# Who requests the first loads, on which queue and in which type, in a one-core convolution and gated FFN kernel

## The chip, the cores and the metric

The kernel runs on one core of a Trainium2 chip. The metric is device time in microseconds (us), lower is better. A core has five engines with instruction streams of their own: TensorE (PE in the profile, its weight loads PEld), VectorE (DVE), ScalarE (ACT), GpSimd (POOL) and SyncE (SP). Transfers between memory and the core are requested by SP, ACT or POOL. Only POOL's requests convert fp32 to fp16 on the way in this kernel; what SP or ACT brings arrives as fp32.

## The reference

A softmax over 7 taps for each of 8 heads, a causal convolution over the sequence with these taps (24 channels a head), and a gated feed-forward layer:

```python
batch, seq, d_model = (8, 4096, 192); kernel_size = 7; n_heads = 8; d_ff = 1536
w = softmax(weight, axis=-1)                       # [8, 7]
x_pad = zeros of 6 rows ahead of x
out[b, s, h, g] = sum_k w[h, k] * x_pad[b, s + k, h, g]
x = out.reshape(32768, 192)
return (np.maximum(x @ w_gate, 0.0) * (x @ w_val)) @ w_out
```

## The kernel before

The batch is cut into two halves, the two *streams*, which are worked on side by side. The sequence is walked in 16 units of 1024 tokens a stream, each of two windows of 512. For each window `gate_val` loops over 12 chunks f of the hidden width: matmuls with the gate and value weights (line 562), relu on ACT (L573), the product on DVE (L574). Then `project` or `project_across` multiplies by `Wo` (L591, L675). PE is meant to run without a break.

The convolution of most units is made on DVE, ACT and POOL beside PE's work. That of the first unit's first window has nobody to hide behind and is made on PE: `conv_dense` (L382) multiplies rows of x with *bands*, matrices that hold the taps along a diagonal. This start is what the change is about. All of it is written out by hand; the program order of each engine is the order of the code.

The start, in the order of its parts:

- *Taps.* `wr` (8 x 7) is loaded. DVE takes the negated maximum (`mx`, L261), ACT the exponentials (`ex`, L264; a `spare` exponential at L144 loads the function table earlier), DVE the sum, its reciprocal and `soft` (L274 to L278). A matmul (L297) spreads `soft` over 112 rows, DVE multiplies it with a 0/1 mask `same` into `diag` (L307), and 14 matmuls with the 0/1 matrix `places` (L317) put the taps where the bands need them. DVE casts the bands from PSUM (`fill_band`, L347), in four pieces for heads 0 to 2, 3, 4 to 5 and 6 to 7. The masks come from `steps`, an iota of POOL, by shifts on DVE (`bits`, L250; `r_of`, L287).
- *x.* The first group has, for each stream, a block of first rows and a body of four pieces of 112 rows (`body`). The first stream's body (L131) and both streams' first rows (L132) come through SP as fp32 into a staging area (`stage`, in the buffer named `prods`) and are cast by ACT (L330, L148) and DVE (L148) into `x_h`. The second stream's body (L138) comes through POOL and is cast on the way.
- *Weights.* `load_w(s)` requests slice s of gate and value weights through POOL, as fp16, into the lower 64 partitions. The upper 64 get a copy (`both_halves`, L183): slices 0 and 1 by DVE, 2 to 5 by POOL (`pool_parts`, `pool_halves`). Slice 5 serves f = 9 to 11.
- *Warm-up.* `warm_up` issues matmuls of constants (L160) of the given widths, whose results nobody reads, to keep PE busy until x and the bands are there.

Of the kernel before, what the change touches and what calls it, by code (L numbers as in the profile page):

```python
# [8 lines left out]
FP = mybir.dt.float32  # L9
# [4 lines left out]
ALU = mybir.AluOpType  # L14
# [3 lines left out]
def kernel(  # L18
# [65 lines left out]
    def load_x(g):  # L84


        bp, toks = GROUPS[g]
        n, rows, step = len(toks), SUB if g < 2 else 128, toks[1] - toks[0]
        xt = xts[g] = x_room()
        for st in range(2):  # L90
            src = bass.AP(
                tensor=x.tensor,
                offset=x.offset + ((bp + NB * st) * S + toks[0] - PAD) * D,
                ap=[[D, rows], [step * D, n], [1, D]],
            )
# [11 lines left out]
    SEG = 16  # L107
    NSEG = SUB // SEG
    wr = const.tile([H, KW], FP)
    nc.sync.dma_start(out=wr[:], in_=weight)  # L110
# [13 lines left out]
    def body(st):  # L124
        return bass.AP(
            tensor=x.tensor,
            offset=x.offset + (NB * st * S + FIRST - PAD) * D,
            ap=[[D, SUB], [DSUB * D, GSUB - 1], [1, D]],
        )
# [5 lines left out]
            tensor=x.tensor, offset=x.offset, ap=[[D, FIRST], [NB * S * D, 2], [1, D]]  # L135
        ),
    )
    nc.gpsimd.dma_start(out=xts[0][0:SUB, 1:GSUB, 1, :], in_=body(1))  # L138
    steps = const.tile([SUB, 64], I32)
    nc.gpsimd.iota(steps[:], pattern=[[1, 64]], base=0, channel_multiplier=64)  # L140
    ones = const.tile([H, 1], FP)
# [1 line left out]
    spare = const.tile([H, 1], FP)  # L143
    nc.scalar.activation(spare[:], ones[:], ACTF.Exp)  # L144
    nc.vector.memset(stage(0, PAD, 0, 2, 0, 1), 0.0)

    def first_rows(copy, cols):
        copy(  # L148
# [9 lines left out]
    def warm_up(*widths):  # L158
        for n, w in enumerate(widths):
            nc.tensor.matmul(  # L160
                out=warm[:, n % 2, 0:w], lhsT=busy[:, 0:128], rhs=busy[:, 0:w], start=True, stop=True
            )

    warm_up(512, 512, 512, 512, 512, 512, 128)

# [4 lines left out]
    Wo = const.tile([128, NFF, D], F16)  # L170
    CUTS = [0, 128, 384, 640, 896, 1152, DFF]

    def load_w(s, which=3):
        cols = slice(CUTS[s], CUTS[s + 1])
        for src, dst in ((moe_w_gate, Wg), (moe_w_val, Wv))[which == 2 : 1 + (which > 1)]:
            nc.gpsimd.dma_start(
                out=dst[0:64, :, cols],
                in_=src.rearrange("(c p) f -> p c f", p=64)[:, :, cols],
            )

    def both_halves(copy, s, dst):
        cols = slice(CUTS[s], CUTS[s + 1])
# [19 lines left out]
    def lane_load(v, hold=None):  # L202


        xe = epool.tile([128, TILES, 2, NCH, 64], F16, name="x_e")
        xes[v] = xe
        for j0, n, t in pieces(v):
            bp, t0 = t // S, t % S
            start = int(t0 == 0)
            if start:  # L210
                nc.gpsimd.memset(xe[0:HALO, j0, :, :, :], 0.0)
            for st in range(2):
                b = bp + NB * st
                first = nc.gpsimd.dma_start(  # L214
                    out=xe[:, j0 + start : j0 + n, st, :, :].rearrange("p j c r -> p j (c r)"),
                    in_=bass.AP(
                        tensor=x.tensor,
                        offset=x.offset + (b * S + t0 - HALO + 128 * start) * D,
                        ap=[[D, 128], [128 * D, n - start], [1, D]],
                    ),  # L220
                )
                if hold is not None:
                    tc.add_manual_dep(first.ins, hold.ins.name, SYNC, reason="behind the turns of the lane before")
                    hold = None
                if start:
# [7 lines left out]
    load_w(1)  # L233
    load_w(2)
    load_rest(load_x(1))
    load_w(3)
    pool_parts(2)
    load_w(4)
    load_w(5)
    pool_halves(3)  # L240
    lane = lane_load(1)
    next(lane)

    ex = const.tile([H, KW + 1], FP)
    nc.vector.memset(ex[:, KW : KW + 1], 1e-9)

# [1 line left out]
    def bits(src, n, down, keep):  # L248
# [8 lines left out]
        )  # L257
        return out

    mx = const.tile([H, 1], FP)  # L260
    nc.vector.tensor_reduce(  # L261
        out=mx[:], in_=wr[:], axis=mybir.AxisListType.X, op=ALU.max, negate=True
    )
    nc.scalar.activation(ex[:, 0:KW], wr[:], ACTF.Exp, bias=mx[:])  # L264
    NROW = SEG + KW - 1
    s_of = bits(steps[:, 0:1], 1, 6, SEG - 1)
    col = bits(steps[:, 0:NROW], NROW, 0, 63)
# [1 line left out]
    with nc.allow_low_precision("zero and one"):  # L269
        nc.vector.tensor_tensor(  # L270
            out=same[:], in0=col[:, 0:SEG], in1=s_of[:].to_broadcast([SUB, SEG]), op=ALU.is_equal
        )
    sm = const.tile([H, 1], FP)
    nc.vector.tensor_reduce(out=sm[:], in_=ex[:], axis=mybir.AxisListType.X, op=ALU.add)  # L274
    nc.vector.reciprocal(sm[:], sm[:])
    soft = const.tile([H, KW, SEG], F16)
    with nc.allow_low_precision("rounded as the band is"):
# [4 lines left out]
            scalar2=None,  # L282
            op0=ALU.mult,
        )
    k_of = bits(steps[:, 0:1], 1, 10, 7)
    r_of = const.tile([SUB, 1], FP)
    nc.vector.tensor_tensor(out=r_of[:], in0=s_of[:], in1=k_of[:], op=ALU.add)  # L287
    with nc.allow_low_precision("zero and one"):
        nc.vector.tensor_scalar(
            out=places[:, SUB - SEG : SUB - SEG + NROW],  # L290
            in0=col[:],
            scalar1=r_of[:],
            scalar2=None,
            op0=ALU.is_equal,
        )
    spread = psum.tile([128, 2, 512], FP, name="ps")
    nc.tensor.matmul(  # L297
        out=spread[0:SUB, 0, 0:H],
# [2 lines left out]
        start=True,  # L301
        stop=True,
    )
    warm_up(512)
    diag = const.tile([SUB, H, SEG], F16)
    with nc.allow_low_precision("products with one and zero"):
        nc.vector.tensor_tensor(  # L307
# [15 lines left out]
                skip_group_check=True,  # L323
            )

    warm_up(512, 256)

    for c in range(NCH):
        cols = slice(64 * c, 64 * c + 64)
        nc.scalar.copy(  # L330
            out=xts[0][0:ROWS0, 1:GSUB, 0, cols],
            in_=stage(0, ROWS0, 0, 1, 1, GSUB - 1)[:, :, cols],
        )
# [586 lines left out]
```

## Time and profile before

| | |
|---|---|
| median of 3 runs | 761.83 us (761.78 to 762.53) |
| profiled execution, its own time | 761.75 us |
| its span, first to last instruction | 760.0 us |
| PE, DVE, ACT, POOL busy | 756.0, 707.8, 617.9, 404.2 us |
| granted TensorE clock, mean | 1.000 |
| first convolution matmul (L382) starts | 5.57 us |
| first gate matmul (L562) starts | 7.29 us |
| one f step of a later window (18.12 to 19.42) | 1.30 us |

A row of the timeline has the start in us, the duration in us, the engine, the line, the operation, what is written and read, the shapes and how often; in square brackets stands how long the engine was idle before and what ended that. SPq and ACTq are queues for transfers; a transfer's row there is only its issue. The list of DMA issues gives the size of a transfer and the us from its issue to its landing. "+1 forms" means that a group has rows of other shapes in it.

### The profile page before, as it was taken

What the parts mean: (1) busy time and instruction counts of PE and PEld (TensorE: products, weight loads), DVE (VectorE), ACT (ScalarE), POOL (GpSimd) and SP (SyncE); (2) the same over time, 40 slices, a digit from 0 to 9 for tenths busy, and PEclk for the clock granted to TensorE, in tenths of its full rate; (3) what the DMA queues carried; (4) which work ended last, traced back from release to release, by engine and by line L of the source; (5) the groups of instructions that cost most, each with busy time, mean ns of one, the idle gap of its engine ahead of it and who ended that gap; (6) DMA issues with size and microseconds to landing.
All of it is one profiled execution on the core that took longest, in us unless ns stands there. A gap on an engine that the chain in (4) does not pass through costs nothing.

```text
span 760.0 us, 30644 instructions
## 1 busy us (share of the span) xinstructions
PE 756.0 (99%) x13637; PEld 461.6 (61%) x13637; DVE 707.8 (93%) x769; ACT 617.9 (81%) x722; POOL 404.2 (53%) x262
## 2 busy tenths in 40 slices
PE   9999999999999999999999999999999999999998
PEld 5595555555555555556555565666666666666548
DVE  7998999999999999999999999999999999999891
ACT  6787887978879798897988879788798887976671
POOL 8519449094580936819276291863908548091000
PEclk9999999999999999999999999999999999999999
DMA  9969029588395894949659498593957939754832
GB/s 131 119 116 140 13 68 169 150 105 183 94 184 146 99 172 105 199 119 134 167 93 184 119 151 167 87 181 113 170 145 104 187 94 157 146 109 109 185 88 85
DMA packets 231452, 100.41 MB, mean 132 GB/s; under 512 B 185240, under 2 KB 220568, under 8 KB 231320
## 3 DMA queue, kind: packets, MB, share of 16 engines
q1 hardware_dynamic: 190280, 82.93, 53.5%
q0 software_dynamic: 40896, 15.50, 19.6%
q8 instruction: 106, 1.74, 1.0%
q14 instruction: 26, 0.21, 0.1%
q10 hardware_dynamic: 144, 0.03, 0.0%
HBM read 31.48 MB, written 47.19 MB: 104 GB/s over the span
## 4 chain that ended last, share of the span: by engine, by line
PE 99%; POOL 0%; DVE 0%; issue 0%; ACT 0%; POOLq 0%
PE ps L562 66%; PE ps L675 29%; PE ps L591 3%; PE ps L642 1%; PE ps L382 0%; PE ps L160 0%; POOL x_h L138 0%; PE ps L317 0%; PE ps L423 0%; DVE bits L250 0%; DVE soft L278 0%; PE ps L297 0%; POOL steps L140 0%; ACT acc L650 0%; DVE same L270 0%
## 5 line engine op out<-in xcount | busy, mean ns | idle before, releaser
L574 DVE TENSOR_TENSOR hT<-gr,ps 128x1024 f16<-128x1024 f16 (+1 forms) x386 | 469.0, 1216 | 29.7 <-ACT gr L573 3.1
L573 ACT ACTIVATE gr<-ps 128x1024 f16<-128x1024 f32 (+1 forms) x386 | 393.3, 1020 | 100.6 <-PE ps L562 100.4
L510 POOL TENSOR_TENSOR prods<-prods 128x1344 f32<-128x1344 f32 x70 | 213.0, 3043 | 268.8 <-DVE prods L506 265.4
L562 PE MATMUL ps<-xc,Wg 64*64 64x512 f16 (+1 forms) x4320 | 318.8, 376 | 0.0
L562 PE MATMUL ps<-xc,Wv 64*64 64x512 f16 (+1 forms) x4320 | 318.7, 376 | 0.0
L675 PE MATMUL ps<-hT,Wo 64*64 64x512 f16 x4032 | 220.1, 376 | 0.0
L562 PEld LDWEIGHTS <-Wv 64*64 64x64 f16 (+1 forms) x4320 | 149.0, 105 | 99.5 <-issue 0.2
L562 PEld LDWEIGHTS <-Wg 64*64 64x64 f16 (+1 forms) x4320 | 145.0, 106 | 103.8 <-issue 0.6
L675 PEld LDWEIGHTS <-Wo 64*64 64x64 f16 x4032 | 130.4, 107 | 87.2
L534 DVE SCALAR_TENSOR_TENSOR acc<-x_r,tap,acc 128x576 f32<-128x576 f16 x225 | 165.3, 812 | 0.0
L504 ACT ACTIVATE prods<-x_r,tap 128x448 f32<-128x448 f16 x222 | 127.2, 659 | 0.0
L697 ACT COPY x_h<-ps 128x2048 uint16<-128x2048 uint16 x28 | 51.8, 1848 | 8.8 <-PE ps L675 8.8
L214 POOL DMA_DIRECT2D x_e<-in_x_dram x58 | 47.0, 818 | 12.4 <-ACT acc L520 12.2
L484 POOL COPY x_p<-x_e 128x960 f16<-128x960 f16 (+1 forms) x58 | 50.4, 913 | 0.0
L510 POOL TENSOR_TENSOR xc<-prods 128x1344 f16<-128x1344 f32 x14 | 42.6, 3040 | 1.1
L697 POOL COPY y<-x_h 128x2048 uint16<-128x2048 uint16 x14 | 26.6, 1898 | 23.3 <-ACT x_h L753 23.3
L534 DVE SCALAR_TENSOR_TENSOR xc<-x_r,tap,acc 128x576 f16<-128x576 f16 x45 | 34.1, 812 | 0.0
L520 ACT ACTIVATE acc<-x_r,tap 128x576 f32<-128x576 f16 x45 | 31.4, 764 | 0.0
L506 DVE TENSOR_SCALAR prods<-x_r,tap 128x448 f32<-128x448 f16 x70 | 27.6, 447 | 0.0
L591 PE MATMUL ps<-Wo,hT 64*128 64x192 f16 x576 | 24.6, 243 | 0.0
L591 PEld LDWEIGHTS <-hT 64*128 64x128 f16 x576 | 24.0, 94 | 0.4
L753 ACT COPY x_h<-ps 128x512 f32<-128x512 f32 x14 | 8.2, 587 | 10.9 <-ACT x_h L697 5.5
(65 smaller groups left out, 92.5 us busy)
## 6 DMA issues: line engine op xcount, KB each, us to landing
out_dram<-out_s SPq DMA_DIRECT2D x62, 384.0 KB, 3.6
held<-x_h SPq DMA_DIRECT2D x14, 512.0 KB, 3.3
held<-x_h SPq DMA_DIRECT2D x28, 256.0 KB, 3.2
held<-y SPq DMA_DIRECT2D x14, 512.0 KB, 5.0
x_e<-in_x_dram POOLq DMA_DIRECT2D x34, 192.0 KB, 6.4
x_e<-in_x_dram POOLq DMA_DIRECT2D x24, 240.0 KB, 5.1
x_r<-x_p SPq DMA_TRANSPOSE x131, 5.2
out_s<-held SPq DMA_TRANSPOSE x56, 5.5
```

The source lines that it names most:

```text
L214: first = nc.gpsimd.dma_start(out=xe[:, j0 + start : j0 + n, st, :, :].rearrange("p j c r -> p j (c r)"), in_=bass.AP(tensor=x.tensor, off ...
L484: nc.gpsimd.tensor_copy(out=xp[:, j0 : j0 + n, :, st, :], in_=xe[:, j0 : j0 + n, st, :, :])
L504: engine.activation(out=out, in_=in_, func=ACTF.Copy, scale=scale)
L510: nc.gpsimd.tensor_tensor(out=pr[:, 0] if k < KW - 1 else xc[v + 1][:, :, LDVE:UNIT], in0=pr[:, 0], in1=pr[:, k], op=ALU.add,)
L520: nc.scalar.activation(out=accs[v][:, c, :], in_=shifted(v, c, 0, 0), func=ACTF.Copy, scale=tap[:, c, 0:1],)
L534: nc.vector.scalar_tensor_tensor(out=xc[v][:, c, 0:LDVE] if k == KW - 1 else acc[:, c, :], in0=shifted(v, c, k, 0), scalar=tap[:, c, k : k ...
L562: nc.tensor.matmul(out=pss[i][m : m + M, st, :], lhsT=W[64 * st : 64 * st + 64, c, 128 * f + m : 128 * f + m + M], rhs=xcb[64 * st : 64 * ...
L573: nc.scalar.activation(out=gr[:, sts], in_=pss[0][:, sts], func=ACTF.Relu)
L574: nc.vector.tensor_tensor(out=h[:, f, sts], in0=gr[:, sts], in1=pss[1][:, sts], op=ALU.mult)
L591: mm = nc.tensor.matmul(out=outs[q], lhsT=h[64 * r : 64 * r + 64, f, st, 128 * q : 128 * (q + 1)], rhs=Wo[64 * r : 64 * r + 64, f, :], sta ...
L675: mm = nc.tensor.matmul(out=ps[bank][64 * half : 64 * half + 64], lhsT=Wo[64 * r : 64 * r + 64, f, d : d + 64], rhs=hs[w][64 * r : 64 * r ...
L697: copy(out=pt[:], in_=src[:].bitcast(U16).rearrange("p b (t l) -> p b l t", l=2))
```

## The change

The taps' request moves from SP to ACT. The second stream's body moves from POOL, which cast it on the way, to SP, as fp32 into the staging area, and is cast there by ACT in three pieces; of the first stream's body, one piece of three moves from ACT to DVE, and the cast of the first rows on DVE now stands ahead of the bands. POOL's first weight request gets a wait for the taps' maximum. The masks and `places` stand ahead of that maximum on DVE. Three warm-ups change their widths.

```diff
-    nc.sync.dma_start(out=wr[:], in_=weight)
+    nc.scalar.dma_start(out=wr[:], in_=weight)
...
-    nc.gpsimd.dma_start(out=xts[0][0:SUB, 1:GSUB, 1, :], in_=body(1))
+    nc.sync.dma_start(out=stage(0, SUB, 1, 1, 1, GSUB - 1), in_=body(1))
...
+    def first_x(copy, st, c0, c1):
+        copy(
+            out=xts[0][0:ROWS0, 1:GSUB, st, 64 * c0 : 64 * c1],
+            in_=stage(0, ROWS0, st, 1, 1, GSUB - 1)[:, :, 64 * c0 : 64 * c1],
+        )
...
-    warm_up(512, 512, 512, 512, 512, 512, 128)
+    warm_up(512, 512, 512, 512, 512, 512, 384)
...
-    def load_w(s, which=3):
+    def load_w(s, which=3, hold=None):
...
-            nc.gpsimd.dma_start(
+            first = nc.gpsimd.dma_start(
...
+            if hold is not None:
+                tc.add_manual_dep(first.ins, hold.ins.name, SYNC, reason="behind the first x")
+                hold = None
...
-    load_w(0)
+    top = nc.vector.tensor_reduce(
+        out=mx[:], in_=wr[:], axis=mybir.AxisListType.X, op=ALU.max, negate=True
+    )
+    nc.scalar.activation(ex[:, 0:KW], wr[:], ACTF.Exp, bias=mx[:])
+    load_w(0, hold=top)
...
-    warm_up(512)
+    warm_up(512, 128)
...
-    warm_up(512, 256)
-
+    warm_up(512)
+
+    first_x(nc.scalar.copy, 0, 0, 1)
+    first_rows(nc.scalar.copy, slice(0, 64))
+    first_x(nc.scalar.copy, 0, 2, 3)
     for c in range(NCH):
-        cols = slice(64 * c, 64 * c + 64)
-        nc.scalar.copy(
-            out=xts[0][0:ROWS0, 1:GSUB, 0, cols],
-            in_=stage(0, ROWS0, 0, 1, 1, GSUB - 1)[:, :, cols],
-        )
-        if c == 0:
-            first_rows(nc.scalar.copy, cols)
+        first_x(nc.scalar.copy, 1, c, c + 1)
+    first_x(nc.vector.tensor_copy, 0, 1, 2)
+    first_rows(nc.vector.tensor_copy, slice(64, D))
...
     fill_band(1, [4, 5], nc.vector.tensor_copy)
-    first_rows(nc.vector.tensor_copy, slice(64, D))
     fill_band(1, [6, 7], nc.vector.tensor_copy)
```

How the instructions stand, at three places. First DVE, from the product `diag` to the first weight copy. Before (`band` is cast from the PSUM tile `ps`, `prods` is the staging area):

```order
L307 TENSOR_TENSOR diag<-ps,same 112x128 [waits PE_49]
L347 CAST band_188<-ps 128x336 [waits PE_49]
L347 CAST band_190<-ps 128x112
L347 CAST band_192<-ps 128x224 [waits PE_49]
L148 CAST x_h<-prods 102x2x128 [waits DMAHW2_49]
L347 CAST band_195<-ps 128x224
L183 COPY Wg<-Wg 64x3x128 [waits DMASW1_49]
```

DVE, the same place now:

```order
L316 TENSOR_TENSOR diag<-ps,same 112x128 [waits PE_49]
L148 CAST x_h<-prods 110x4x64 [waits DMAHW1_49]
L154 CAST x_h<-prods 102x2x128 [waits DMAHW2_49]
L355 CAST band_192<-ps 128x336 [waits PE_49]
L355 CAST band_194<-ps 128x112
L355 CAST band_196<-ps 128x224 [waits PE_49]
L355 CAST band_198<-ps 128x224
L192 COPY Wg<-Wg 64x3x128 [waits DMASW0_49]
```

A cast of the first body is new, and it and the first rows' cast, each behind a transfer of SP's, stand ahead of all four bands.

Second POOL, from the start of the program. Before:

```order
L138 DMA x_h<-in_x_dram 112x4x192
L140 ISA
L140 IOTA steps 112x64
L176 DMA Wg<-in_moe_w_gate_dram 64x3x128
L176 DMA Wv<-in_moe_w_val_dram 64x3x128
L176 DMA Wg<-in_moe_w_gate_dram 64x3x256
```

POOL, the same place now:

```order
L140 ISA
L140 IOTA steps 112x64
L182 DMA Wg<-in_moe_w_gate_dram 64x3x128 [waits DVE_49]
L182 DMA Wv<-in_moe_w_val_dram 64x3x128
L182 DMA Wg<-in_moe_w_gate_dram 64x3x256
```

The body's transfer is gone from the head of the queue, and the first weight request waits for DVE, with all that follows on POOL behind it.

Third ACT, from the start of the program to the first casts of PSUM. Before:

```order
L144 ACT_TABLE_LOAD
L144 ACTIVATE spare<-ones 8x1 [waits DVE_49]
L264 ACTIVATE ex<-wr,mx 8x7 [waits DMAHW0_49,DVE_49]
L330 CAST x_h<-prods 110x4x64 [waits DMAHW1_49]
L148 CAST x_h<-prods 102x2x64 [waits DMAHW2_49]
L330 CAST x_h<-prods 110x4x64 x2
L400 CAST xc<-ps 128x512 [waits PE_49] x2
```

ACT, the same place now:

```order
L110 DMA wr<-in_weight_dram 8x7
L144 ACT_TABLE_LOAD
L144 ACTIVATE spare<-ones 8x1 [waits DVE_49]
L280 ACTIVATE ex<-wr,mx 8x7 [waits DMAHW0_49,DVE_49]
L148 CAST x_h<-prods 110x4x64 [waits DMAHW1_49]
L154 CAST x_h<-prods 102x2x64 [waits DMAHW2_49]
L148 CAST x_h<-prods 110x4x64
L148 CAST x_h<-prods 110x4x64 [waits DMAHW3_49]
L148 CAST x_h<-prods 110x4x64 x2
L407 CAST xc<-ps 128x512 [waits PE_49] x2
```

The taps' request stands ahead of the table load, and three casts of the second stream's body, behind SP's third transfer, ahead of the first `xc`.

More of the change, by code (lines that the diff above doesn't have):

```diff
@@ L230, in lane_load @@
                 yield
-    load_w(0)
[L233 to L242, printed above, removed]
     ex = const.tile([H, KW + 1], FP)
@@ L258, in bits @@
         return out
-    mx = const.tile([H, 1], FP)
-    nc.vector.tensor_reduce(
-        out=mx[:], in_=wr[:], axis=mybir.AxisListType.X, op=ALU.max, negate=True
-    )
-    nc.scalar.activation(ex[:, 0:KW], wr[:], ACTF.Exp, bias=mx[:])
     NROW = SEG + KW - 1
@@ L272 @@
         )
+    k_of = bits(steps[:, 0:1], 1, 10, 7)
+    r_of = const.tile([SUB, 1], FP)
+    nc.vector.tensor_tensor(out=r_of[:], in0=s_of[:], in1=k_of[:], op=ALU.add)
+    with nc.allow_low_precision("zero and one"):
+        nc.vector.tensor_scalar(
+            out=places[:, SUB - SEG : SUB - SEG + NROW],
+            in0=col[:],
+            scalar1=r_of[:],
+            scalar2=None,
+            op0=ALU.is_equal,
+        )
+    mx = const.tile([H, 1], FP)
+    top = nc.vector.tensor_reduce(
+        out=mx[:], in_=wr[:], axis=mybir.AxisListType.X, op=ALU.max, negate=True
+    )
+    nc.scalar.activation(ex[:, 0:KW], wr[:], ACTF.Exp, bias=mx[:])
+    load_w(0, hold=top)
+    load_w(1)
+    load_w(2)
+    load_rest(load_x(1))
+    load_w(3)
+    pool_parts(2)
+    load_w(4)
+    load_w(5)
+    pool_halves(3)
+    lane = lane_load(1)
+    next(lane)
     sm = const.tile([H, 1], FP)
@@ L284 @@
         )
[L285 to L295, printed above, removed]
     spread = psum.tile([128, 2, 512], FP, name="ps")
@@ L324 @@
             )
-    warm_up(512, 256)
+    warm_up(512)
+    first_x(nc.scalar.copy, 0, 0, 1)
+    first_rows(nc.scalar.copy, slice(0, 64))
+    first_x(nc.scalar.copy, 0, 2, 3)
     for c in range(NCH):
-        cols = slice(64 * c, 64 * c + 64)
-        nc.scalar.copy(
-            out=xts[0][0:ROWS0, 1:GSUB, 0, cols],
-            in_=stage(0, ROWS0, 0, 1, 1, GSUB - 1)[:, :, cols],
-        )
-        if c == 0:
-            first_rows(nc.scalar.copy, cols)
+        first_x(nc.scalar.copy, 1, c, c + 1)
+    first_x(nc.vector.tensor_copy, 0, 1, 2)
+    first_rows(nc.vector.tensor_copy, slice(64, D))
     bands, wide_bands, ends = {}, {}, []
```

## The prediction

> **What bounds the kernel now.** I read the page first: the share of each engine and the chain that ended last.
>
> ```profile
> PE 756.0 (99%) x13637; PEld 461.6 (61%) x13637; DVE 707.8 (93%) x769; ACT 617.9 (81%) x722; POOL 404.2 (53%) x262
> PE 99%; POOL 0%; DVE 0%; issue 0%; ACT 0%; POOLq 0%
> ```
>
> TensorE (PE) carries 99% of the chain, so a change counts only if it moves PE's first useful matmul or opens a gap behind it. The timeline shows both ends of that question: the first convolution matmul (L382), and the pace of the gate and value matmuls (L562) afterwards.
>
> ```profile
> 5.57 1.78 PE L382 MATMUL ps<-band,x_h 110*32 110x104 f16 x120
> 18.12 0.81 PE L562 MATMUL ps<-xc,Wg 64*128 64x512 f16 x6
> 19.42 0.81 PE L562 MATMUL ps<-xc,Wg 64*128 64x512 f16 x6
> ```
>
> One step of the f loop takes 19.42 - 18.12 = 1.30 us for six pairs of 512 columns, 0.22 us a pair, and nothing else stands between. The edits lie wholly before about 21 us, so the time follows the start of L382 (5.57) and any new gap in the next 16 us. What could be won in all is little: no step shown below ends early enough to let L382 start before about 5.4.
>
> What feeds L382? The timeline of each engine, in order of time:
>
> ```profile
> 0.74 0.41 SPq L110 DMA_DIRECT2D wr<-in_weight_dram  x1
> 0.74 1.28 ACT L144 ACT_TABLE_LOAD   x1 [0.74 <-PEq L904]
> 1.21 0.34 SPq L131 DMA_DIRECT2D prods<-in_x_dram  x1
> 1.31 0.88 POOL L138 DMA_DIRECT2D x_h<-in_x_dram  x1 [0.87 <-POOLq L904]
> 1.36 0.06 DVE L245 MEMSET ex<- 8x1 f32 x1
> 1.59 0.48 SPq L132 DMA_DIRECT2D prods<-in_x_dram  x1
> 2.03 0.20 ACT L144 ACTIVATE spare<-ones 8x1 f32<-8x1 f32 x1
> 2.10 0.15 DVE L261 TENSOR_REDUCE mx<-wr 8x1 f32<-8x7 f32 x1 [0.67 <-DMA wr<-in_weight_dram]
> 2.28 0.30 ACT L264 ACTIVATE ex<-wr,mx 8x7 f32<-8x7 f32 x1
> 2.28 0.22 POOL L140 IOTA steps<- 112x64 int32 x1
> 2.41 0.68 POOL L176 DMA_DIRECT2D Wg<-in_moe_w_gate_dram  x1
> 2.53 0.24 DVE L250 TENSOR_SCALAR bits<-steps 112x1 int32<-112x1 int32 x2 [0.29 <-POOL steps L140]
> 2.81 0.17 DVE L270 TENSOR_TENSOR same<-bits,bits 112x16 f16<-112x16 int32 x1
> 2.90 0.14 DVE L274 TENSOR_REDUCE sm<-ex 8x1 f32<-8x8 f32 x1
> 3.26 0.32 DVE L278 TENSOR_SCALAR soft<-ex,sm 8x112 f16<-8x112 f32 x1
> 3.51 0.13 DVE L250 TENSOR_SCALAR bits<-steps 112x1 int32<-112x1 int32 x1
> 3.63 0.25 PE L297 MATMUL ps<-same,soft 8*112 8x8 f16 x1
> 3.82 0.61 PE L160 MATMUL ps<-const-bfloat16-1.0 128*128 128x512 bf16 x1
> 4.02 0.28 DVE L307 TENSOR_TENSOR diag<-ps,same 112x128 f16<-112x128 f32 x1
> 4.35 0.91 PE L317 MATMUL ps<-diag,places 112*128 112x64 f16 x14
> 4.59 0.41 ACT L330 CAST x_h<-prods 110x256 f16<-110x256 f32 x1 [2.01 <-DMA prods<-in_x_dram]
> 4.92 0.51 DVE L347 CAST band<-ps 128x336 f16<-128x336 f32 x1 [0.62 <-PE ps L317]
> 5.10 0.30 ACT L148 CAST x_h<-prods 102x128 f16<-102x128 f32 x1
> 5.83 0.45 DVE L148 CAST x_h<-prods 102x256 f16<-102x256 f32 x1
> ```
>
> Three things must be there. The first band is written by 4.92 + 0.51 = 5.43. The casts of the first stream's x on ScalarE (ACT) end at 5.10 + 0.30 = 5.40. The second stream's x comes through GpSimd's (POOL's) cast transfer, whose landing the list of DMA issues gives:
>
> ```profile
> x_h<-in_x_dram POOLq DMA_DIRECT2D x1, 168.0 KB, 4.3
> prods<-in_x_dram SPq DMA_DIRECT2D x1, 144.0 KB, 3.5
> ```
>
> Issued at 1.31 it lands at about 1.31 + 4.3 = 5.6, just where L382 starts. Softmax, staged x and second x thus end within 0.2 us of each other; taking one away uncovers the next.
>
> **The change part by part.** *Requests.* With the taps gone from SyncE's (SP's) queue, the first body goes out at 0.74 instead of 1.21. The first rows follow 0.38 us later (1.59 - 1.21), at 1.12, and the second body at about 1.12 + 0.48 + 0.04 = 1.65, behind both. The first body landed 4.59 - 1.21 = 3.4 us after its issue, so now at 4.1; the first rows at 1.12 + 3.5 = 4.6. For the second body the nearest rows give 1.65 + 3.4 = 5.05 at best and, at POOL's 4.3, 5.95 at worst. I take 5.15, nearer SP's rows, because it is now the same kind of transfer on the same queue, as a volume check bears out:
>
> ```profile
> 3.00:3.50 0.50, 0.50 (x3) 0.02 (x1) 0.43 (x3) 0.00 (x0) 0.50 (x2) 1.00 1.07 362
> 4.00:4.50 0.50, 0.50 (x5) 0.25 (x5) 0.30 (x2) 0.00 (x0) 0.50 (x2) 1.00 1.44 226
> 4.50:5.00 0.50, 0.50 (x13) 0.50 (x12) 0.08 (x1) 0.41 (x1) 0.50 (x2) 1.00 1.61 191
> ```
>
> The last column is GB/s. The x transfers run at 362 once they flow, near 3.0, or 2.5 with the requests 0.47 earlier. All three together are 336 + 144 + 336 = 816 KB, 0.84 MB, or 2.3 us at that rate: done at 4.8, plus some tenths to be reported.
>
> The Trainium skill (DMA: Bandwidth & Descriptors, "Issuing engines are not separate DMA queues") speaks against the move: transfers of all issuers run on the same 16 engines, and another issuer saves only issue time. By that, the fp32 second body, twice the bytes written, would gain nothing from its new queue, and the sum would come to case C below.
>
> *Taps' chain.* On ACT the request (0.41, the SP row's) stands ahead of the table load: 0.74 + 0.47 = 1.21, + 1.28 + 0.20 = 2.7 for the end of `spare`. On POOL the iota loses the 0.88 us transfer ahead of it and ends at about 1.5 if it starts where that transfer did. On VectorE (DVE) the bits, `same`, second bits, `r_of` and `places` come ahead of the maximum: 2.53 to 2.98, and 3.51 to 4.02, which is 0.45 + 0.5 = 0.95 us; started at 1.42 to 1.6, they end at 2.4 to 2.55. The maximum (0.15; the taps having landed at 2.10, if ACT's queue is as quick as SP's) ends at 2.55 to 2.7. So `ex` starts at 2.7, not 2.28. From `ex`'s end to `soft`'s end takes 3.58 - 2.58 = 1.0 in the trace, but 0.32 of it was DVE busy with `bits` and `same` (2.58 to 2.90), so now 0.68 + 0.02: `soft` ends at 2.7 + 0.3 + 0.7 = 3.7 instead of 3.58. Of the 0.42 us lost at `ex`, 0.3 is given back.
>
> *Bands.* L297's matmul moves to 3.74, and the 512-column warm-up 0.19 behind it. Those 512 columns take 0.43 us at the slow clock and the added 128 another 0.11, so L317's place matmuls start near 3.93 + 0.54 = 4.47, not 4.35: +0.12. `diag` stays hidden (about 4.05 to 4.33). DVE then has two casts in place of one before the first band: the x cast (256 elements, like the 0.45 us row at 5.83, which takes 0.37 of DVE before the next starts) from 4.36, the first rows from 4.73 (landed at 4.6), done at 5.1; PSUM is ready at 4.92 + 0.12 = 5.04. So the band is cast from 5.1 to 5.6. Both casts are hidden by 0.06 us short of all; if the first rows land late, every tenth counts in full.
>
> *ACT's casts.* First piece 4.12, rows 4.65, third piece 4.95, then the second stream's first piece from 5.25 to 5.65. L382 starts at about 5.65: **+0.08**. The rest of these casts and bands are due later, at 0.6 us for each third of L382.
>
> *Weights.* The first weight issue waits for the maximum: 2.6 to 2.75 instead of 2.41, **+0.2 to +0.35**, and everything queued behind it on POOL moves with it: six weight transfers, x of the next group, the half copies. Who waits for POOL last is seen here:
>
> ```profile
> 20.09 1.16 POOL L183 COPY Wv<-Wv 64x1152 f16<-64x1152 f16 x1
> 21.15 0.53 PEld L562 LDWEIGHTS <-Wv 64*128 64x128 f16 x6
> ```
>
> The copy ends at 21.25, in the middle of the weight loads that use it: no cover. POOL late by 0.2 to 0.35 against PE late by 0.08 leaves 0.1 to 0.27; against it stands the second body's cast, gone from POOL's stream. I take **+0.12**. Below nothing the weights bring no gain, as PE is then full.
>
> *Sum.* +0.08 + 0.12 = +0.2 us. The profiled execution took 761.75 (span 760.0 and 1.75 around it), 0.08 under the median of 761.83. So 761.95 by that execution, **762.0** as a median.
>
> **The rivals.** *A, forecast (0.55):* as summed, 762.0.
>
> *B, a small gain (0.20).* PE is let through as soon as `diag` is there, the casts hide, and the lighter POOL stream keeps the half copies on time: band at 4.92, L382 at 5.43 to 5.45. That is -0.12, up to -0.3 with less loss inside the block: 761.6.
>
> *C, x late (0.12).* One SP queue now holds all of it. At 226 GB/s, the rate of the rows in which weights run beside x, 0.84 MB takes 3.7 us from 2.5: 6.2, plus the 0.41 cast, L382 at 6.65: +1.1, 762.9. At the 191 of the next row it is 6.9 and +1.75. It decides once the second body lands after 5.25. Against it: the hold keeps the weights out until then. With the landing at 5.95, from POOL's row, L382 would start near 6.4, for 762.7. The section of the Trainium skill named above (DMA: Bandwidth & Descriptors) is the rule behind this case.
>
> *D, the clock comes late (0.10), slower.* The lines by form show when PE speeds up, though the granted clock column says 1.00 throughout:
>
> ```profile
> L160 PE MATMUL ps<-const-bfloat16-1.0 128*128 128x512 bf16 x1 | 0.6, 607 | 0.0
> L160 PE MATMUL ps<-const-bfloat16-1.0 128*128 128x512 bf16 x1 | 0.5, 461 | 0.0
> ```
>
> The 512-column matmul at 3.82 took 607 ns, the one at 5.07 461: the switch falls near 5.2, 4.4 us after the first warm-up (0.78). If the wait ahead of L297 starts this anew, 4.4 us from 3.9 is 8.3; work from 5.65 to 8.3 at half pace costs 1.3 us: 763.1 to 763.3. It is beyond 0.2% if full pace comes after 8.7, to which I give half of this chance. For it: the wait moves; against it: the warm-up grows from 128 to 384 columns just there (0.21 us at the slow pace), covering the 0.11 us move.
>
> The Trainium skill (TensorE: Matmul & The Clock Gate, "Part 1: The HAM clock gate") has the clock follow a free-running window of some 3.4 us of activity. By that, the switch could only slip by a whole window, 5.2 to 8.6, for an estimated 1.5 us and 763.4; no row here shows the window itself.
>
> *E, the edits do nothing (0.03).* If POOL's first instruction comes so late that the weights would go out at 2.6 anyway, the hold is empty and all covers hold: 761.8.
>
> **How the numbers follow.** The likeliest case gives 762.0. The range runs from B's far end (761.5), less 0.2 since each landing in it is known to a tenth or two, to D's first price: 761.3 to 763.1. Left out are C's worse end and half of D, about 0.1. For this kernel 0.2% is 1.5 us, about what a measurement can tell from no change: 760.3 to 763.35. Slower by more needs the late half of D (0.05), C at 191 GB/s (0.04), or something unpriced (0.04): 0.13. Faster by more would need L382 at 4.05, before the first body has landed: 0.02. The rest, 0.85, lies within.
>
> **What the profile after would show.** Right: L382 starts at 5.55 to 5.75, its release an ACT cast of the second stream or a band; the maximum at 2.4 to 2.55 and the first weights at 2.6 to 2.75; the last value weights' copy ending near 21.5 with a small gap on PE; one f step still 1.30. Wrong: the second body landing after 5.3 (C), the last warm-up ahead of L382 still at 607 ns for 512 columns (D), or PE gaps beyond 22 us, of which I foresee none.

## The result: slower by 0.22%

The changed kernel took 763.93 us (median of 13 runs, 762.94 to 766.0), the kernel before 762.33 beside it (13 runs, 761.78 to 763.23): ratio 1.0022, interval 1.0015 to 1.0029, or 1.1 to 2.2 us. Forecast were 762.0 and a range up to 763.1. The profiled execution took 763.40, with a span of 761.6.

The page of the changed kernel, its first line of busy time and the chain that ended last:

```profile
PE 756.7 (99%) x13637; PEld 492.0 (65%) x13637; DVE 708.5 (93%) x770; ACT 618.6 (81%) x724; POOL 403.0 (53%) x261
PE 99%; DMA 1%; SPq 0%; ACT 0%; issue 0%
```

TensorE still carries the chain, but ahead of it stands a transfer where before stood POOL's iota and DVE's masks. PE's waits over the first 25 us say where it stood still; the kernel before has only the first 0.8 of the program's start:

```profile
PE ps L389 <- ACT x_h L148: 0.8, 1, 0.8
PE ps L166 <- PEq L911: 0.8, 1, 0.8
PE ps L389 <- DVE band L355: 0.2, 1, 0.2
```

The timeline after, in order of time; most lines have moved by 6 to 10 (L389 is the convolution, L569 the gate and value matmuls, L192 the copies of the weights):

```profile
0.74 0.59 ACTq L110 DMA_DIRECT2D wr<-in_weight_dram  x1
0.74 0.39 SPq L131 DMA_DIRECT2D prods<-in_x_dram  x1
1.19 0.48 SPq L132 DMA_DIRECT2D prods<-in_x_dram  x1
1.71 0.45 SPq L138 DMA_DIRECT2D prods<-in_x_dram  x1
2.22 0.14 DVE L277 TENSOR_REDUCE mx<-wr 8x1 f32<-8x7 f32 x1
2.65 0.20 ACT L144 ACTIVATE spare<-ones 8x1 f32<-8x1 f32 x1
2.67 0.81 POOL L182 DMA_DIRECT2D Wg<-in_moe_w_gate_dram  x1 [1.65 <-DVE mx L277]
2.76 0.28 ACT L280 ACTIVATE ex<-wr,mx 8x7 f32<-8x7 f32 x1
3.45 0.32 DVE L298 TENSOR_SCALAR soft<-ex,sm 8x112 f16<-8x112 f32 x1
4.63 0.41 ACT L148 CAST x_h<-prods 110x256 f16<-110x256 f32 x1 [1.59 <-DMA prods<-in_x_dram]
5.18 0.29 DVE L154 CAST x_h<-prods 102x256 f16<-102x256 f32 x1 [0.25 <-DMA prods<-in_x_dram]
5.27 0.45 PE L166 MATMUL ps<-const-bfloat16-1.0 128*128 128x512 bf16 x1
5.39 1.28 DVE L355 CAST band<-ps 128x336 f16<-128x336 f32 x4
5.94 0.22 PE L389 MATMUL ps<-band,x_h 110*32 110x104 f16 x2 [0.22 <-DVE band L355]
6.54 1.02 ACT L148 CAST x_h<-prods 110x256 f16<-110x256 f32 x3 [0.76 <-DMA prods<-in_x_dram]
7.00 1.54 PE L389 MATMUL ps<-band,x_h 110*32 110x104 f16 x118 [0.83 <-ACT x_h L148]
8.47 0.39 PE L569 MATMUL ps<-xc,Wg 64*128 64x512 f16 x2
```

Two matmuls of the convolution go at 5.94, and then PE waits for ACT's first cast of the second body, which starts as soon as that body has landed. The chain has it as one piece:

```profile
1.71 4.81 DMA prods<-in_x_dram
6.54 0.41 ACT x_h L148
```

Requested at 1.71, landed at 6.52, cast 0.41 us long: the other 118 matmuls start at 7.00, and the first gate matmul at 8.47 instead of 7.29, which is +1.18. A little more is lost just behind it. The timeline of DVE and of PE's weight loads:

```profile
9.65 0.97 DVE L192 COPY Wv<-Wv 64x768 f16<-64x768 f16 x1
10.67 0.33 PEld L569 LDWEIGHTS <-Wv 64*128 64x128 f16 x5 [0.37 <-DVE Wv L192]
11.99 0.33 PEld L569 LDWEIGHTS <-Wv 64*128 64x128 f16 x6 [0.34 <-DVE hT L581]
```

and DVE's copy in the kernel before:

```profile
8.62 0.40 DVE L183 COPY Wv<-Wv 64x768 f16<-64x768 f16 x1
```

That copy took 0.40 us before, and POOL's own copy began only behind it (9.11). Begun later, it takes 0.97 beside POOL's copy (9.52 to 10.34). The weight load waits 0.37 for it, and another one waits 0.34 for the product `hT`, which stands behind the copy on DVE. At f = 5 the distance is 1.45. At the last `project` it is 1.71, and in the two executions' own times 1.65. The growth from 1.45 to 1.71 comes in steps too small for the profile to show a wait of PE's (none beyond 25 us); its cause is open.

### The profile page after: what moved, and what is told of

The parts are those of the page before. It is cut to its first block, busy times and chain, and to the rows that moved or that the text cites. A ratio compares the mean times of both kernels' runs of the same rounds, so it can differ in the third digit from the quotient of the medians.

```text
span 761.6 us, 30645 instructions
## 1 busy us (share of the span) xinstructions
PE 756.7 (99%) x13637; PEld 492.0 (65%) x13637; DVE 708.5 (93%) x770; ACT 618.6 (81%) x724; POOL 403.0 (53%) x261
## 4 chain that ended last, share of the span: by engine, by line
PE 99%; DMA 1%; SPq 0%; ACT 0%; issue 0%
PE ps L569 65%; PE ps L682 29%; PE ps L598 3%; PE ps L649 1%; DMA prods<-in_x_dram 1%; PE ps L389 0%; PE ps L430 0%; SPq L132 0%; ACT x_h L148 0%; SPq L131 0%; ACT acc L657 0%
## 5 line engine op out<-in xcount | busy, mean ns | idle before, releaser
L569 PE MATMUL ps<-xc,Wg 64*64 64x512 f16 (+1 forms) x4320 | 323.1, 376 | 0.0
L569 PE MATMUL ps<-xc,Wv 64*64 64x512 f16 (+1 forms) x4320 | 322.8, 376 | 0.0
L569 PEld LDWEIGHTS <-Wg 64*64 64x64 f16 (+1 forms) x4320 | 156.8, 106 | 92.0 <-issue 0.6
L569 PEld LDWEIGHTS <-Wv 64*64 64x64 f16 (+1 forms) x4320 | 154.1, 105 | 95.0 <-issue 0.9
L682 PEld LDWEIGHTS <-Wo 64*64 64x64 f16 x4032 | 143.9, 107 | 73.6
```

What stands on the lines that cost most here:

```text
L569: nc.tensor.matmul(out=pss[i][m : m + M, st, :], lhsT=W[64 * st : 64 * st + 64, c, 128 * f + m : 128 * f + m + M], rhs=xcb[64 * st : 64 * ...
L682: mm = nc.tensor.matmul(out=ps[bank][64 * half : 64 * half + 64], lhsT=Wo[64 * r : 64 * r + 64, f, d : d + 64], rhs=hs[w][64 * r : 64 * r ...
```

## The experiments

Theory V: the loss is the second body as fp32. It is the last of 816 KB on the wire and has a cast behind it. Its rivals are the queue, the taps' place, the weights beside x, and a fixed delay of a third request. Each edit is shown against the kernel named.

**The second body back on POOL, ahead of the iota** (against after; ACT's three casts of it go too).

```diff
-    nc.sync.dma_start(out=stage(0, SUB, 1, 1, 1, GSUB - 1), in_=body(1))
+    nc.gpsimd.dma_start(out=xts[0][0:SUB, 1:GSUB, 1, :], in_=body(1))
```

> The changed kernel with one edit undone: the second stream's body goes back to GpSimd's queue, cast on the way, with its three ScalarE casts gone. Theory V (volume: the second body as fp32, last of 816 KB of x, lands at 6.5, and that alone is the loss): the convolution starts at 5.6 to 5.9 instead of 7.0 for its third matmul, and the time is 1.2 to 1.7 us under the changed kernel's, ratio to before 0.9995 to 1.0008. Rival O (the other edits, taps on ScalarE, two casts ahead of the bands, the weights' hold, cost as much): the ratio stays at 1.0015 or more.

764.13 us against 761.92, ratio 1.0026 (1.0015 to 1.0036): no better than after. That is rival O's ratio, but the trace gives another reason. The iota stands behind the 0.88 us request again (2.29), while DVE now has the masks ahead of the maximum; so `soft` ends at 4.6 and the matrix product behind it starts at 4.68, after 0.87 us of idle time on PE. The convolution then starts without a wait for x, but runs at PE's slow pace (a 512-column matmul ahead of it takes 0.61 us, not 0.38):

```profile
6.68 2.57 PE L387 MATMUL ps<-band,x_h 110*32 110x104 f16 x120
```

The next kernel starts its 118 main matmuls at the same time (6.66) and takes 1.54 us for them. So what this kernel loses against it, 1.06 us at the first gate matmul, is the slow pace, which lasts until about 8.9. That the 0.87 us of idle time caused it is likely but not shown. The next kernels keep the iota first.

**The same behind the iota** (against after; ACT's three casts of it go too, the hold and all else are kept).

```diff
-    nc.sync.dma_start(out=stage(0, SUB, 1, 1, 1, GSUB - 1), in_=body(1))
     nc.gpsimd.iota(steps[:], pattern=[[1, 64]], base=0, channel_multiplier=64)
+    nc.gpsimd.dma_start(out=xts[0][0:SUB, 1:GSUB, 1, :], in_=body(1))
```

> The changed kernel with the second body back on GpSimd's queue, cast on the way, but behind the iota, so that masks, maximum and weights' hold keep their new places and times (the first undoing moved the iota too, and with it the whole chain of the taps). Theory V: the iota ends at 1.0, the maximum near 2.35, the body is requested at 1.35 and lands at 5.6 to 6.1; the convolution runs without a gap from 5.8 to 6.1, and the time is 0.7 to 1.4 us under the changed kernel's, ratio to before 1.000 to 1.0013. Rival O (the other edits carry the loss even with the iota early): ratio 1.0015 or more.

762.78 against 762.22, ratio 1.0004 (0.9995 to 1.0012). This gives back most of the loss: the intervals of this kernel and of after do not touch. DMA issue and timeline:

```profile
x_h<-in_x_dram POOLq DMA_DIRECT2D x1, 168.0 KB, 5.2
6.66 1.54 PE L387 MATMUL ps<-band,x_h 110*32 110x104 f16 x118 [0.56 <-DMA x_h<-in_x_dram]
```

The body lands at 1.43 + 5.2 = 6.63, no earlier than in after and not at the expected 5.6 to 6.1, although only half of the bytes are written. But there is no cast between it and PE: 6.66, not 7.00. What is left against before (0.56 us in the medians) goes with the late landing; the kernels with the taps on ACT and on SP, below, say where it comes from.

**Queue or type: POOL's queue, but fp32 and ACT's casts** (against after).

```diff
-    nc.sync.dma_start(out=stage(0, SUB, 1, 1, 1, GSUB - 1), in_=body(1))
     nc.gpsimd.iota(steps[:], pattern=[[1, 64]], base=0, channel_multiplier=64)
+    nc.gpsimd.dma_start(out=stage(0, SUB, 1, 1, 1, GSUB - 1), in_=body(1))
```

> As the run above, on GpSimd's queue behind the iota, but as fp32 into the staging area with the three ScalarE casts: only the type on the way differs. If the type (336 KB written instead of 168 KB, and a cast behind the landing) carries the loss, the body lands 0.3 us or more later than the cast transfer does and the ratio is at least 1.001 above that run's. If the queue carries it (rival Q), both runs give the same time within 0.4 us.

763.69, ratio 1.0023 (1.0013 to 1.0034): the time of after, with another queue. DMA issue and timeline:

```profile
prods<-in_x_dram POOLq DMA_DIRECT2D x1, 336.0 KB, 5.0
6.96 1.54 PE L389 MATMUL ps<-band,x_h 110*32 110x104 f16 x118 [1.04 <-ACT x_h L148]
```

It lands at 1.45 + 5.0 = 6.45, 0.2 before the fp16 body and not 0.3 or more behind it as expected, and ends PE's wait at 6.96. So the type decides and not the issuer, and it does so by the cast: a body that arrives as fp16 saves the 0.41 us behind the landing. Writing half of the bytes did not make it land earlier.

**The fp32 body alone** (against before; requested by SP as the third, three casts on ACT behind the others, no hold, old order).

```diff
-    nc.gpsimd.dma_start(out=xts[0][0:SUB, 1:GSUB, 1, :], in_=body(1))
+    nc.sync.dma_start(out=stage(0, SUB, 1, 1, 1, GSUB - 1), in_=body(1))
```

> The kernel before with one edit alone: the second stream's body through SyncE as fp32 into the staging area, behind the taps, the first body and the first rows, and three ScalarE casts of it behind the first stream's. Theory V: the body is requested near 2.2 and lands at 6.5 to 7.2, the third convolution matmul starts 0.4 behind that, ratio 1.0015 to 1.003. Rival O: the ratio is under 1.0008. Rival W (the weights' cast transfers beside it slow it): without the hold it lands later than 7.2, ratio over 1.002.

765.67 against 761.92, ratio 1.0047 (1.0032 to 1.0061): this one edit loses more than the whole change. Its PE timeline:

```profile
7.35 1.70 PE L388 MATMUL ps<-band,x_h 110*32 110x104 f16 x118 [1.69 <-ACT x_h L338]
8.98 0.61 PE L568 MATMUL ps<-xc,Wg 64*128 64x512 f16 x2
```

The body, requested at 2.11 behind the taps, lands at 6.9, within the forecast of V; the time is above it (1.003 at most), as the gate matmuls then run at 0.61 us, not 0.39. PE has lost its full pace as well: the profile's granted clock is 0.50 from 8.6 to 12.0.

**The taps on ACT alone** (against before).

```diff
-    nc.sync.dma_start(out=wr[:], in_=weight)
+    nc.scalar.dma_start(out=wr[:], in_=weight)
```

> The kernel before with one edit: the taps' request on ScalarE's queue, so that SyncE's two x requests go out 0.47 us earlier. Theory V (what counts is when the last of the first x lands and what is cast behind it; the fp16 body keeps 0.5 MB of x on the wire): the fp16 body is still requested near 1.3 by GpSimd and lands at 5.6 to 5.9, the convolution starts at 5.5 to 5.8, median within 0.5 us of before. Rival T (the earlier requests of SyncE push GpSimd's body behind them; that is why the fp16 body landed 0.6 us later in the two runs with the change's requests): the body lands at 6.2 or later, a PE wait of 0.5 us or more at the first convolution, median +0.5 to +1 us.

763.13 against 762.32, ratio 1.0013 (1.0005 to 1.0022). DMA issue and timeline:

```profile
x_h<-in_x_dram POOLq DMA_DIRECT2D x1, 168.0 KB, 4.8
6.01 2.90 PE L382 MATMUL ps<-band,x_h 110*32 110x104 f16 x120
```

Two things happen. ACT's table load is pushed back, so `ex` starts at 2.76 instead of 2.28, the first band at 5.11 instead of 4.92, and the convolution, behind its warm-ups, at 6.01 instead of 5.57. And SP's x, requested 0.47 earlier, delays POOL's body: 4.8 us to landing instead of 4.3, so 6.1 instead of 5.6. In this execution PE also kept its slow pace until about 10.2 (the convolution took 2.90 us, not 1.78), so its profile (763.89) is worse than its median. How much of the median is pace and how much the two delays is not shown.

**All but the taps** (against after: the taps' request back on SP, ahead of the bodies).

```diff
-    nc.scalar.dma_start(out=wr[:], in_=weight)
+    nc.sync.dma_start(out=wr[:], in_=weight)
```

> The kernel after, with the taps' request back on SyncE ahead of the bodies; all x stays fp32 on SyncE. Theory V (the volume of 0.84 MB in fp32 and the cast behind it): all x requests go out 0.41 to 0.47 us later, the second body lands 0 to 0.4 us later than 6.52, at 6.5 to 6.9, median as after or up to 0.5 us above. Rival T (the taps' place is what loses the time): the median comes back to before by 0.5 us or more.

765.09, ratio 1.003 (1.0018 to 1.0041; it overlaps that of after, but the trace shows where it goes). Chain and PE's timeline:

```profile
2.11 5.67 DMA prods<-in_x_dram
8.26 2.51 PE L389 MATMUL ps<-band,x_h 110*32 110x104 f16 x118 [1.93 <-ACT x_h L148]
```

0.40 us later in its request, the body lands 1.26 later (7.78; expected was 6.9 at the latest): its last 122 packets go after 5.5 us, beside the weights that are still requested at 2.67; in after only 17 do. The convolution also runs mostly at a granted clock of 0.50 (8.6 to 12.0), which costs it 0.97 us more (2.51 against 1.54). So in these traces the taps' move helps the changed kernel, and alone it hurts: what it gives SP's transfers it takes from POOL's.

**All but the hold** (against after).

```diff
-    load_w(0, hold=top)
+    load_w(0)
```

> The kernel after, without the hold: the first weights are requested from about 1.05 instead of 2.67, at the same time as SyncE's x. Theory V: the weights share the 16 engines with x from the start, and x lands later: the second body at 6.8 to 7.5, median 0.3 to 1 us above after; the hold is then the part of the change that does help. Rival N (the hold is without effect, since x goes first anyway): landed at 6.5, median as after within 0.2 us.

765.96 against 762.43, ratio 1.0051 (1.0036 to 1.0066), clear of after's interval: the hold is worth some 2 us to the changed kernel. Chain and PE's timeline:

```profile
1.71 6.13 DMA prods<-in_x_dram
8.32 1.93 PE L389 MATMUL ps<-band,x_h 110*32 110x104 f16 x84 [2.41 <-ACT x_h L148]
```

The view ends at 10 us, so its row has 84 of the 118 matmuls. With the first weights requested at 1.37 the body lands at 7.84, 1.32 later than in after. Much of the rest of the loss is again the clock, 0.50 from 8.4 to 11.8.

**A longer hold** (against after: the weights' requests wait for ACT's first cast of the second body, and POOL's calls move behind it in the code).

```diff
-    load_w(0, hold=top)
+    load_w(0, hold=held[0])
```

> The changed kernel with the weights' wait moved behind the first ScalarE cast of the second body, so that no weight transfer runs beside x. Rival W (the weights' transfers beside it slow the second body): it lands at 5.5 or sooner. Theory V (x alone): it lands at 6.1 to 6.5 as in the changed kernel. The weights come too late in any case, so the time itself is 2 us or more over the changed kernel's.

768.82 in a single run, as the weights are far too late. But the body still lands at 1.71 + 4.6 = 6.3: taking the weights off the wire beyond what the hold does buys 0.2 us. They are not what is left of the loss.

**The second body on ACT's queue, first of all** (against after; the taps back on SP).

```diff
-    nc.sync.dma_start(out=stage(0, SUB, 1, 1, 1, GSUB - 1), in_=body(1))
+    nc.scalar.dma_start(out=stage(0, SUB, 1, 1, 1, GSUB - 1), in_=body(1))
```

> The changed kernel with the requests of taps and second body exchanged: the body goes on ScalarE's queue at 0.74, the taps on SyncE's ahead of the first body. Same bytes, another queue, requested 1.0 us earlier. Theory V (bytes on shared engines set the landing): the three x transfers share the engines, the second body lands at 5.5 to 6.5 and the first body later than 4.6; the time stays within 0.5 us of the changed kernel's. Rival Q (third place on one queue sets the landing): the second body lands at 4.6 to 5.2, the convolution starts at 5.9 to 6.0 with the bands, and 0.8 to 1.1 us of the loss is gone.

764.99 against 761.92, ratio 1.004 (1.0024 to 1.0055). The DMA view of 2.0 to 3.5 us, by queue (q10 is ACT's, q1 SP's):

```profile
q10 hardware_dynamic: 443, 0.33, 74.5%
q1 hardware_dynamic: 86, 0.07, 12.9%
```

In this stretch the two queues hardly run side by side. ACT's packets go first, SP's wait, though SP's request is only 0.47 us behind: now the first body lands at 5.7 and the first rows at 6.3 (before: 4.6 and about 5.1), and the bands behind their casts start the convolution at 7.16. After 2.04 us of idle time it runs at a granted clock of 0.50 until 10.5, which V had not expected (it put the time within 0.5 us of after's). No gain came from the other queue.

**SP's order changed: the rows last** (against after).

```diff
+    nc.sync.dma_start(out=stage(0, SUB, 1, 1, 1, GSUB - 1), in_=body(1))
     nc.sync.dma_start(out=stage(PAD, FIRST, 0, 2, 0, 1), ...)
-    nc.sync.dma_start(out=stage(0, SUB, 1, 1, 1, GSUB - 1), in_=body(1))
```

> The kernel after, with SyncE's order changed: first body, second body, first rows. Theory V (SyncE's transfers are served in turn, and the last of 816 KB lands at about 6.5 whichever it is): the second body lands near 5.6 to 5.9, the first rows now near 6.5, and the casts that wait for the rows (also ahead of the bands on VectorE) hold the bands and the convolution's start to 6.8 or later: median as after or slower by up to 0.8 us. Rival F (the second body is slow because of its own place as the third request of a queue, with a fixed latency): body 2 lands 0.5 us earlier and rows only 0.3 later, median 0.5 us under after.

764.84, ratio 1.0033 (1.002 to 1.0046). The chain shows the rows as the last to land:

```profile
1.71 4.28 DMA prods<-in_x_dram
6.02 0.29 DVE x_h L154
```

They land at 5.99, 0.5 earlier than the second body did in that place and than V expected, but all four bands stand behind their cast:

```profile
6.78 2.94 PE L389 MATMUL ps<-band,x_h 110*32 110x104 f16 x120 [0.90 <-DVE band L355]
```

The convolution thus starts 0.22 before the 7.00 of after, and the time is still worse, because it runs at the slow pace (2.94 us against 1.54), which here lasts until about 10.0. So the order of the loads decides what PE waits for, but the time above that of after is pace.

**Half of the second body** (against after: 168 of its 336 KB, the rest filled with zeros by POOL).

```diff
-    nc.sync.dma_start(out=stage(0, SUB, 1, 1, 1, GSUB - 1), in_=body(1))
+    nc.sync.dma_start(out=stage(0, SUB, 1, 1, 1, 2), in_=half)
```

> The kernel after, with only two of the second body's four pieces brought in (168 KB instead of 336; the other two are filled with zeros by GpSimd before its first weight request, so half of the second stream's first window is left out of the convolution). Theory V (landing is set by the volume of x on the wire, some 330 packets of 768 B a microsecond by then): 224 packets fewer, 0.6 to 0.7 us earlier: landed at 5.8 to 5.95 instead of 6.52, the convolution goes on at 6.25 to 6.4 instead of 7.00, median 0.6 us under after. Rival F (a delay of the third request that doesn't hang on its size): landed at 6.4 or later, median as after within 0.2 us.

761.97 against 762.43, ratio 0.9998 (0.9988 to 1.0007): the loss is gone. DMA issue and timeline:

```profile
prods<-in_x_dram SPq DMA_DIRECT2D x1, 168.0 KB, 3.7
5.67 1.83 PE L396 MATMUL ps<-band,x_h 110*32 110x104 f16 x120 [0.43 <-DVE band L362]
```

Landed at 5.41, 1.11 us earlier, more than the 0.6 to 0.7 that V gave it, and the casts are done before PE gets there. A fixed delay is out; the amount of fp32 x ahead of the last landing is the cause (bytes and packets were halved together, so the two are not told apart). It also bounds what is to be won: even with a fifth of the first x left out (168 of 816 KB), this start only ties with the kernel before. No version was found that beats it.

**What is left of the change without the fp32 body.** Three kernels take the pieces apart further. After with the body on POOL as fp16 behind the iota, and no hold:

```diff
-    nc.sync.dma_start(out=stage(0, SUB, 1, 1, 1, GSUB - 1), in_=body(1))
     nc.gpsimd.iota(steps[:], pattern=[[1, 64]], base=0, channel_multiplier=64)
+    nc.gpsimd.dma_start(out=xts[0][0:SUB, 1:GSUB, 1, :], in_=body(1))
...
-    load_w(0, hold=top)
+    load_w(0)
```

> The run with the iota first, without the weights' wait for the maximum: the weights are requested right behind the body, near 2.2. Theory V: x comes first in GpSimd's queue anyway, so the hold gives nothing there; same time within 0.3 us, or 0.1 to 0.3 us less, since the weights come earlier. Rival W: the body lands later by 0.3 us or more and the time is longer.

763.01, ratio 1.0005 (0.9996 to 1.0014); the body lands at 6.42 and PE waits 0.54 us for it. Before with only the iota ahead of POOL's body:

```diff
-    nc.gpsimd.dma_start(out=xts[0][0:SUB, 1:GSUB, 1, :], in_=body(1))
     nc.gpsimd.iota(steps[:], pattern=[[1, 64]], base=0, channel_multiplier=64)
+    nc.gpsimd.dma_start(out=xts[0][0:SUB, 1:GSUB, 1, :], in_=body(1))
```

> The kernel before with one edit: GpSimd's iota ahead of its first x transfer. The taps' maximum (2.10, the taps' landing) then sets the masks' chain, soft ends near 3.3 instead of 3.58, the bands near 5.1 instead of 5.4, while the second body still lands at 5.6: the time is that of before within 0.2 us, since that landing already set the start.

762.03 against 762.22, ratio 1.0000 (0.9991 to 1.0009); the body lands at 5.83, the convolution starts at 5.64. And the first of these two with the taps back on SP:

```diff
-    nc.scalar.dma_start(out=wr[:], in_=weight)
+    nc.sync.dma_start(out=wr[:], in_=weight)
```

> The kernel after, with the second body back on GpSimd's casting queue behind the iota, no hold, and the taps back on SyncE ahead of the x requests: of the change only the new order on VectorE and ScalarE, the warm-ups and the iota's place are left. Rival T: the body lands at 5.8 as in the kernel before with the iota first, the convolution's wait of 0.54 us is gone, median at before or up to 0.4 us under it. Theory V without T: landing stays near 6.4, median +0.4 us as with the taps on ScalarE.

762.56, ratio 1.0004 (0.9995 to 1.0012). DMA issue and timeline:

```profile
x_h<-in_x_dram POOLq DMA_DIRECT2D x1, 168.0 KB, 4.4
6.04 1.57 PE L387 MATMUL ps<-band,x_h 110*32 110x104 f16 x120 [0.40 <-DVE band L353]
```

The body lands at 5.84, so it was the taps' place that made it 0.6 late (5.0 us to landing with the taps on ACT, 4.4 with them on SP, as in the kernel with only the iota moved). But PE's wait has only changed its name: it is now for the bands, which stand behind two casts of x on DVE, the first of them released at 4.96 by SP's body.

## Why the prediction was wrong

*Failed: the landing of the second body.* "I take 5.15, nearer SP's rows" was 6.52. Its support, the volume check, had the right bytes and two wrong terms. The DMA view by queue, after, for 2.5 to 3.5 us and then 3.5 to 4.5, and for 5.5 to 6.0:

```profile
q1 hardware_dynamic: 420, 0.31, 100.6%
...
q1 hardware_dynamic: 330, 0.24, 110.5%
...
q1 hardware_dynamic: 17, 0.01, 7.6%
```

and before, for 3.0 to 4.0:

```profile
q1 hardware_dynamic: 490, 0.36, 107.8%
```

The columns behind the queue are packets, MB and the share of 16 engines' time. Flow did begin near 2.5. But the 362 GB/s of before (0.36 MB in a microsecond) were not held: after moved 0.31 MB in its first microsecond and 0.24 in the next. In before a packet took 1.078 x 16 / 490 = 35 ns of an engine, in after 38 ns at first and then 1.105 x 16 / 330 = 54 ns, with no packet of the weights on the wire yet (their first goes at 4.6). So the last packet of x went near 5.7 and not 4.8. And "some tenths to be reported" were 0.8 us, from there to 6.52. Together 0.9 + 0.5 above the forecast. The second term could have been read in the kernel before: SP's last packet there goes near 4.3, and its rows land at 5.1.

*The cast behind it* was in the forecast (0.41), but as hidden: "L382 starts at about 5.65" has it from 5.25. With the landing at 6.52 it lies on the path in full, so the +0.08 for the start of the convolution was +1.43 for all but its first two matmuls.

*Right on the path, too low in chance: case C* ("x late", 0.12). It named the place, the order of waits and the point from which it decides (landing after 5.25), and gave +1.1 to +1.75; the profiled executions differ by 1.65. That the size fits is in part luck. Its rates, 226 and 191 GB/s, were read as x with weights beside it. The queue that ran beside SP's in these two rows was POOL's, before, 4.0 to 4.5 and 4.5 to 5.0:

```profile
q0 software_dynamic: 172, 0.07, 109.3%
...
q0 software_dynamic: 258, 0.10, 160.7%
```

These packets are of 384 bytes (0.07 MB in 172), and 448 of them make the 168 KB of the second body: mostly x, cast on the way. In after the rate first fell without any such neighbour. C left no time for the report. And of the 1.65 only 1.18 is there at the first gate matmul; the rest arose behind it. The row that was weighed against it, SP's 3.4 to 3.5 us for 336 and 144 KB, was of a queue with 480 KB on it, and the request that came last on a full wire was priced with it. The Trainium skill (DMA: Bandwidth & Descriptors, "Issuing engines are not separate DMA queues") was cited as speaking against the move; the kernels with the fp32 body on ACT's and on POOL's queue agree with it, as neither is faster: 764.99 and 763.69 against 763.93.

*Wrong: the first body would land at 4.1*, from its request 0.47 earlier. It landed at 4.62, as before: 3.9 us after the request, not 3.4. The rows' 4.6 was 5.16 for the same reason, so DVE's x cast waited, the bands came at 5.39 and not 5.1, and PE waited 0.22 for the first: "every tenth counts in full" was right.

*Right: the taps' chain.* `ex` at 2.76 (forecast 2.7), `soft`'s end at 3.77 (3.7), the first weights at 2.67 (2.6 to 2.75). Only the maximum was ready early (2.36, not 2.55 to 2.7): ACT's table load and `spare` behind it are what hold `ex`.

*Wrong in sign: POOL's +0.12.* The last copy of the value weights did not come later:

```profile
19.63 1.16 POOL L192 COPY Wv<-Wv 64x1152 f16<-64x1152 f16 x1
```

It ends at 20.79, before: 21.25, while PE had moved back by 1.45. What PE lost behind the convolution (0.27 by f = 5) came from DVE's copy, which the forecast did not look at.

*Case D* did not happen in the profiled execution (the last 512-column warm-up took 0.45 us, as before at 0.46). But it is real in the experiments: full pace came only near 8.9, 10.0 and 10.2 us in three of them, and in five it came and was lost again. *B* and *E* are out: nothing started earlier, and the hold is worth 2 us.

## What to carry to other kernels

Price a transfer by its place on the wire, not by the row of an earlier one: add up the bytes requested ahead of it on every queue, and take the rate and the report of the last one, not of the first. Check in the view by queue whose packets a rate belongs to. An edit that brings a transfer forward moves another one back, so price both; here the taps' move helped SP's transfers and hurt POOL's. And when a cast moves from the transfer to an engine, it is hidden only if the transfer is not the last to arrive.

## What the runs showed of the hardware

- Packets of the same size (768 bytes of x on SP's queue) took 35 to 38 ns of an engine at first and 54 ns later in the changed kernel, with all 16 engines' time taken in both. It also happens with the half body (468 packets from 2.5 to 3.5 us, then 312) and with the longer hold, where no weights are on the wire (449, then 304). In the kernel before, with 480 KB on this queue, it does not happen. Why is not settled.
- From the last packet of x on SP's queue to its landing took 0.7 us before (4.3 to 5.1), 0.8 after (5.7 to 6.5) and 1.1 without the hold (6.7 to 7.84).
- PE falls back to a slower pace after a wait, and such a wait is paid twice. In five kernels the profile's granted clock drops to 0.50 during the convolution or just behind it. In four of them it stays there for 3.4 us: 8.6 to 12.0 with the fp32 body alone and with the taps on SP, 8.4 to 11.8 without the hold, 7.1 to 10.5 with the body on ACT's queue; with the longer hold it drops at 7.1 and PE then waits for weights. In all five the matmuls had come to full pace 3.4 us before the drop (5.2, 5.2, 5.0, 3.7, 3.7). In these 3.4 us PE had idled for 1.36 us (0.80 + 0.56, the longer hold) or more. With 1.05 idle (0.22 + 0.83, after) and 1.04 (POOL's queue, fp32) full pace stayed: the convolution's 118 matmuls took 1.54 us and the first gate matmuls 0.39. The Trainium skill (TensorE: Matmul & The Clock Gate, "Part 1: The HAM clock gate") has the pace follow PE's activity in windows of some 3.4 us. By that, a pace gained near 5.2 could be lost near 8.6 and regained near 12.0, and the kernel with the taps on SP agrees: its warm-up at 5.18 is at full pace (0.38), its convolution from 8.26 mostly slow, and its gate matmuls are back at 0.39 from 11.96.
- The first full pace can come late as well: near 8.9 with 0.87 us of idle time ahead of it (the body back on POOL, ahead of the iota), near 10.0 with 0.90 (the rows last), and near 10.2 with only 0.21 (the taps alone on ACT). The last is not explained. The granted clock reads 1.00 in all three up to there, so this slow pace shows only in the durations (0.61 us for a 512-column matmul, not 0.38).
